# Linear attention feeding a SoLU layer on one core: the hand-written order of 907 pieces replaced by another

## The chip, the cores and the metric

The kernel runs on one core of one Trainium2 chip. What counts is the device time of one execution in microseconds (us). The core's engines each work through a queue of their own, in order: TensorE (PE in the profile, its weight loads PEld), VectorE (DVE), ScalarE (ACT), GpSimd (POOL) and SyncE (SP, which here only issues transfers). Transfers run on 16 DMA engines, whoever issues them.

## The reference

```python
q, k, v: (8, 8, 576, 64)            # batch, heads, sequence, head_dim, float32
kv  = einsum('bhsd,bhse->bhde', k, v)
o   = einsum('bhsd,bhde->bhse', q, kv)
a   = o / sqrt(mean(o * o, -1) + 1e-6) * g_norm
x   = a.transpose(0, 2, 1, 3).reshape(4608, 512)
h   = x @ w_in                      # 512 -> 1024
sm  = exp(h - max h) / (sum + 1e-9)
u   = h * sm                        # SoLU
ln  = (u - mean u) / sqrt(var u + 1e-6) * g_ln
out = ln @ w_out                    # 1024 -> 512, float32
```

## The kernel before, in words

The 4608 tokens are cut into nine chunks of 512. Chunk c from 0 to 7 holds eight of each nine tokens of batch c; chunk 8 gathers the ninth ones of all batches (`q_last`). The work on every chunk is cut into small pieces with names such as `h.3.5.0`; the first number is the chunk, or the batch.

The attention pieces: `kv_mm` (L375, PE) multiplies k by v, and `kv` copies (L229) bring the result from PSUM to SBUF in three parts, one of them whole and two shifted by half the partitions. `qT_mm` (L427, PE) turns q, and `qT` copies it out; from chunk 4 on, `qT` is instead one transposing transfer that SP issues (L435). `o_mm` (L448, PE) multiplies the turned q by kv, for two halves `hf` of the heads. `sq` (L233, ACT) squares o, `oa` (L460) adds two quarters of the squares, `s_mm` (L465, PE) averages them over a head, `ln` and `ex` (L472 and L476, ACT) make one over the root of it (for chunk 0 a single `ex`, L482), and `x` (L489, DVE, two instructions each) multiplies o by this and by g_norm.

The SoLU pieces: `h` (L532, PE) is a product with a slice of 128 columns of w_in, four matmuls of 512 columns. For chunks 0 to 2 it comes in two pieces of two matmuls (called halves below), so that the first can run when half of x is there. `exp` (L539, ACT) and `u` (L543, DVE, h times exp h) follow; no maximum is subtracted, and the division by the sum of exps is folded into the final scaling. `usq` (L233 on ACT or L235 on POOL) squares u, `es` (L551, POOL) adds two e. `ua`, `usqa` and `esa` (L575, DVE) fold eight slices of u, of its squares, and the four of es, to fewer; `sums` (L594, PE) adds what is left over the columns; `turn`, `stats` (L601 to L611, DVE) and `rstd` (L615, L617, ACT) make the scaling of each token. `out` (L651, PE) is the product with w_out, which has been centered once (`w_mean` on PE, `w_center` on DVE, L632 and L638). `ob` (L239 on ACT, L241 on DVE) scales it out of PSUM, and `store` brings it to memory: 256 KB a piece. The last piece, `out.8.3`, is done by halves of its columns (L659).

`warm` pieces (L300, PE) are products of zeros that nobody reads; `WARM` tells how many matmuls each has.

Nothing schedules this but the text in `ORDER`: `Plan.emit` takes its words one by one and emits the piece, so every engine gets its instructions in the order of the words. A word may name the engine (`:act`, `:pool`); without it a piece goes to the first engine allowed for it: DVE for `kv`, `qT`, `oa` and `ob`, POOL for `usq` and `es`, SP for `store`. The digits of `ROOMS` tell which of the 8 PSUM banks, or which SBUF buffer, each tile takes, in the order of first use; a tile waits until all users of the one before it in that room are done. `Plan.run` adds waits of its own:

```python
        if engine == "pool":
            self.after(ins, self.adds)
            self.adds.clear()
        if name[0] in ("ua", "usqa", "esa", "oa") and engine == "dve":
            self.adds.append(ins)
        elif name[0] in ("k", "v", "q", "q_last", "w_in", "w_out") and engine == "pool":
            self.after(ins, self.turns)
            ...
        elif name[0] == "qT" and engine == "sp":
            self.after(ins, self.loads[-2:-1])
```

So a piece on POOL waits for the adds of DVE that stand ahead of it in the order, a load issued by POOL for the transposing transfers ahead of it, and a transposing transfer for a load.

Loads of q, k, v and the weights are issued by POOL, which converts to bfloat16 on the way (L322, L338, L343, L348). Half of batch 0's v and k comes as float32 through SP (`wide`, L328) and is converted by ACT (`v.0.1`, `k.0.1`). `ident` (POOL) builds the unit matrices for the turns.

Of the kernel before, what the change touches and what calls it, by code (L numbers as in the profile page):

```python
# [30 lines left out]
u.0.7 sq.1.1.0 es.0.3 h.0.5.1 u.0.4 sq.1.1.1 h.1.0.0 w_mean.0 usq.0.1:act oa.1.1 u.0.0 exp.0.5 s_mm.1.1 ln.1.1 ex.1.1
u.0.5 es.0.2 w_mean.1 w_mean.2 w_mean.3 w_mean.4 w_mean.5 w_mean.6 usq.0.5:act x.1.1.1 usq.0.2 usq.0.7:act w_mean.7
x.1.1.0 usq.0.0 q.4.0 usq.0.4:act w_center.5 h.1.3.0 qT_mm.2.1 h.1.7.0 w_center.1 h.1.4.0 h.1.7.1 qT.2.1:act q.5.0
w_center.4 h.1.0.1 v.4.0 w_center.0 exp.1.7 qT_mm.2.0 exp.1.0 w_center.3 h.1.1.0 h.1.1.1 k.4.0 qT.2.0:act w_center.2
h.1.2.1 es.0.1 u.1.7 h.1.3.1 exp.1.1 h.1.4.1 u.1.0 exp.1.3 out.0.2.0 es.1.0 usq.0.3 u.1.1 exp.1.2 out.0.2.1 kv_mm.2.0
w_center.7 exp.1.4 h.1.5.0 w_center.6 kv.2.1.0:act kv.2.0.0:act h.1.5.1 kv.2.0.2:act kv.2.1.1 kv.2.0.1:act es.1.1
u.1.4 out.0.2.2 kv.2.1.2:act exp.1.5 o_mm.2.0 u.1.3 o_mm.2.1 sq.2.0.1 out.0.2.3 usq.1.1 u.1.2 qT_mm.3.0 sq.2.0.0 u.1.5
out.0.0.0 sq.2.1.1 oa.2.0 out.0.0.1 sq.2.1.0 qT.3.0 s_mm.2.0 usq.1.5 out.0.0.2 ln.2.0 qT_mm.3.1 oa.2.1:pool ex.2.0
h.1.6.0 qT.3.1 out.0.0.3 usq.1.2:act x.2.0.0 x.2.0.1 h.1.6.1 s_mm.2.1 exp.1.6 sums.0 usq.1.7 ln.2.1 u.1.6 ex.2.1
# [696 lines left out]
```

## Time and profile before

| | us |
|---|---|
| median of 3 runs | 177.52 (177.48 to 177.98) |
| span of the profiled execution | 175.8 |
| busy: PE, DVE, ACT, POOL | 164.2, 145.5, 152.1, 99.8 |
| DMA | 30.27 MB moved, 172 GB/s in the mean |

The profile is of one execution, in which no time but the span is given; the time of a run is larger than the span by what lies before the first and behind the last instruction (177.52 - 175.8 = 1.7 if that execution took the median). Its lines read: source line, engine, operation, what is written `<-` what is read, the number of instructions, then busy time, mean ns of one, and idle time of the engine ahead of them with what ended it. In the timeline a line begins with start and duration in us. A table of stretches gives for each engine its busy time in the stretch, then the clock granted to TensorE (1.00 is full), the busy share of the DMA engines and the GB/s that they moved. Matmuls overlap in their pipeline, so their durations in the timeline are longer than their distance.

### The profile page before, as it was taken

Reading aid. Unit: us, or ns where it says so; the run is one execution under the profiler, and the core shown is the slowest. Engines: PE = TensorE matmul, PEld = TensorE weight load, DVE = VectorE, ACT = ScalarE, POOL = GpSimd, SP = SyncE. Lnnn points to the kernel's source line nnn. Section 1 sums busy time; section 2 is a strip of 40 time slices with the busy share of each in tenths; the row PEclk is TensorE's granted clock in tenths of the full one; section 3 lists DMA queues with packets and bytes.
Section 4 is the critical chain, followed back from the end, with each engine's and each line's share of the span. In section 5 each row is a group of like instructions: output and inputs, shape, how many; then the busy total and the mean of one; then the engine's idle time right before and its main releaser. Section 6 shows DMA issues by size and latency. Waiting matters only on the chain.

```text
span 175.8 us, 4843 instructions
## 1 busy us (share of the span) xinstructions
PE 164.2 (93%) x1913; PEld 80.3 (46%) x1938; DVE 145.5 (83%) x317; ACT 152.1 (86%) x273; POOL 99.8 (57%) x108
## 2 busy tenths in 40 slices
...
GB/s 179 218 203 214 206 275 373 209 208 208 208 210 210 218 210 129 127 206 235 205 183 259 150 52 193 156 73 93 195 206 105 5 118 126 2 60 93 196 213 159
DMA packets 34623, 30.27 MB, mean 172 GB/s; under 512 B 16288, under 2 KB 28328, under 8 KB 34600
## 3 DMA queue, kind: packets, MB, share of 16 engines
...
q8 instruction: 15, 0.25, 0.6%
...
HBM read 32.51 MB, written 9.44 MB: 239 GB/s over the span
## 4 chain that ended last, share of the span: by engine, by line
PE 75%; DVE 10%; ACT 5%; DMA 5%; issue 2%; POOL 1%; POOLq 0%; DVEq 0%; ACTq 0%
PE h_ps L532 31%; PE out_ps L651 30%; DMA k_sb<-in_k_dram 5%; PE kv_ps L375 4%; PE o_ps L448 3%; DVE u_sb L543 3%; PE sum_ps L594 3%; PE s_ps L465 3%; DVE x_sb L489 2%; DVE w_out_sb L638 2%; ACT osq_sb L233 2%; DVE osq_sb L460 1%; PE out_ps L659 1%; ACT e_sb L539 1%; ACT kvd L229 1%
## 5 line engine op out<-in xcount | busy, mean ns | idle before, releaser
L532 PE MATMUL h_ps<-x_sb,w_in_sb 128*128 128x512 bf16 x280 | 68.0, 379 | 0.5
L651 PE MATMUL out_ps<-w_out_sb,u_sb 128*128 128x512 bf16 x266 | 65.2, 379 | 0.7 <-issue 0.3
L551 POOL TENSOR_TENSOR es_sb<-e_sb 128x512 bf16<-128x512 f32 x36 | 45.4, 1279 | 33.5 <-ACT e_sb L539 13.0
L539 ACT ACTIVATE e_sb<-h_ps,zero_t 128x512 f32<-128x512 f32 x72 | 46.2, 690 | 2.3 <-PE h_ps L532 1.7
L543 DVE TENSOR_TENSOR u_sb<-h_ps,e_sb 128x512 bf16<-128x512 f32 x72 | 46.6, 684 | 1.3 <-ACT e_sb L539 1.0
L532 PEld LDWEIGHTS <-w_in_sb 128*128 128x128 bf16 x288 | 27.3, 98 | 32.5 <-issue 1.3
L651 PEld LDWEIGHTS <-u_sb 128*128 128x128 bf16 x280 | 26.4, 98 | 31.6 <-issue 1.0
L233 ACT ACTIVATE usq_sb<-u_sb,zero_t 128x512 bf16<-128x512 bf16 x49 | 33.6, 718 | 0.0
L489 DVE SCALAR_TENSOR_TENSOR x_sb<-o_ps,g_sb,rst_sb 128x256 bf16<-128x256 f32 x72 | 30.2, 478 | 3.1 <-ACT rst_sb L476 2.5
L235 POOL TENSOR_TENSOR usq_sb<-u_sb 128x512 bf16<-128x512 bf16 x23 | 23.6, 1043 | 7.9 <-DVE osq_sb L460 5.6
L233 ACT ACTIVATE osq_sb<-o_ps,zero_t 128x512 bf16<-128x512 f32 x36 | 22.8, 689 | 3.5 <-PE o_ps L448 3.4
L239 ACT ACTIVATE ob_sb<-out_ps,rstd 128x512 f32<-128x512 f32 x22 | 14.8, 684 | 4.0 <-PE out_ps L651 3.8
L575 DVE TENSOR_TENSOR usq_sb<-usq_sb 128x2048 bf16<-128x2048 bf16 (+2 forms) x20 | 17.0, 848 | 0.6 <-ACT usq_sb L233 0.4
L229 DVE CAST kvd<-kv_ps 64x128 bf16<-64x128 f32 (+3 forms) x26 | 6.4, 256 | 11.2 <-ACT kvd L229 6.5
L241 DVE TENSOR_SCALAR ob_sb<-out_ps,rstd 128x512 f32<-128x512 f32 (+1 forms) x15 | 10.6, 711 | 4.1 <-PE out_ps L659 2.2
L322 POOL DMA_DIRECT2D v_sb<-in_v_dram x9 | 6.8, 757 | 10.1 <-DVE sum_ps L601 2.8
L472 ACT ACTIVATE lss_sb<-s_ps,eps_t 128x512 f32<-128x512 f32 x16 | 11.1, 695 | 1.0 <-PE s_ps L465 0.7
L476 ACT ACTIVATE rst_sb<-lss_sb,zero_t 128x512 f32<-128x512 f32 x16 | 11.5, 722 | 0.4
L375 PE MATMUL kv_ps<-v_sb,k_sb 64*64 64x64 bf16 x576 | 8.0, 194 | 2.8 <-DMA k_sb<-in_k_dram 1.3
L300 PE MATMUL warm_ps<-zeros 128*128 128x512 bf16 x25 | 8.8, 481 | 1.4 <-DVE zeros L255 1.2
L229 ACT CAST kvd<-kv_ps 64x128 bf16<-64x128 f32 (+3 forms) x34 | 8.2, 243 | 2.2 <-PE kv_ps L375 1.5
L375 PEld LDWEIGHTS <-k_sb 64*64 64x64 bf16 x576 | 6.8, 107 | 6.8 <-DMA k_sb<-in_k_dram 2.6
...
## 6 DMA issues: line engine op xcount, KB each, us to landing
...
q_sb<-in_q_dram POOLq DMA_DIRECT2D x6, 512.0 KB, 16.2
...
```

Of the source, the lines that this page charges most:

```text
L229: nc.scalar.copy(dst, src) if engine == "act" else on[engine].tensor_copy(dst, src)
L233: nc.scalar.activation(out=dst, in_=src, func=AF.Square, bias=zero_t[:, :])
L235: on[engine].tensor_tensor(out=dst, in0=src, in1=src, op=MUL)
L239: nc.scalar.activation(out=dst, in_=src, func=AF.Copy, scale=by)
L375: nc.tensor.matmul(t[64 * y:64 * y + 64, :], T["k", b][rows, n, i, :], T["v", b][rows, n, i, :], start=(i == 0 and (b < 2 or m == 0)), sto ...
L489: nc.vector.scalar_tensor_tensor(out=t[:, 2 * hf + dh, z], in0=T["o", c, hf, z][:, dh], scalar=g_rep[dh], in1=T["rst", c, hf][:, z], op0=M ...
L532: nc.tensor.matmul(bank(("h", c, f), [128, 512])[:, :], w_in_sb[:, dt, f * 128:(f + 1) * 128], T["x", c][:, dt].rearrange("p a b c -> p (a ...
L539: nc.scalar.activation(out=t[:, f % 2, :], in_=T["h", c, f][:, :], func=AF.Exp, bias=zero_t[:, :])
L543: nc.vector.tensor_tensor(out=t[:, f, :], in0=T["h", c, f][:, :], in1=T["e", c, f // 2][:, f % 2, :], op=MUL)
L551: on[engine].tensor_tensor(out=t[:, n, :], in0=e[:, 0, :], in1=e[:, 1, :], op=ADD)
L575: nc.vector.tensor_tensor(out=to[:, 0:n, :], in0=src[:, 0:n, :], in1=src[:, n:2 * n, :], op=ADD)
L651: nc.tensor.matmul(bank(("out", c, m), [128, d_model])[:, :], T["u", c][:, f, m * 128:(m + 1) * 128], w_out_sb[:, f, :], start=(f == 0), s ...
```

## The change

The three texts are replaced; the functions stay. The same 907 pieces are emitted in another order, with other rooms. The seven `warm` pieces have 45 matmuls instead of 27. Another engine is named for 73 pieces:

| pieces | from, to | from, to |
|---|---|---|
| `usq` | ACT to POOL 17 | POOL to ACT 11 |
| `kv` copies | ACT to DVE 15 | DVE to ACT 12 |
| `oa` | DVE to POOL 5 | POOL to DVE 1 |
| `ob` | ACT to DVE 4 | DVE to ACT 3 |
| `qT` copies | ACT to DVE 2 | DVE to ACT 1 |
| last stores | `store.8.2` ACT to SP | `store.8.0` SP to ACT |

POOL issues its 40 loads in the same succession, and so does SP its own, but for `store.8.2` in the place of `store.8.0`. `ident` moves behind the first three loads of POOL. The diff, cut to its core (the old order's lines first):

```diff
 ORDER = """
-wide.v ident wide.k g_rows q.0.1 v.0.0 k.0.0 q.0.0 v.0.1:act v.1.0 k.1.0 q.1.0 w_in.0 k.0.1:act w_in.1 warm.0
-kv_mm.0.1.0 qT_mm.0.1 kv.0.1.0.0:act kv.0.1.1.0 kv_mm.0.1.1 q.1.1 qT.0.1:act kv.0.1.2.1 kv.0.1.2.0 kv.0.1.1.1
-kv.0.1.0.1:act warm.1 kv_mm.0.0.0 v.1.1 kv_mm.0.0.1 o_mm.0.1 kv.0.0.0.1 sq.0.1.1 warm.2 qT_mm.0.0 k.1.1 kv.0.0.1.0:act
-kv.0.0.2.0:act kv.0.0.1.1:act kv.0.0.0.0:act qT.0.0 kv.0.0.2.1:act sq.0.1.0 warm.3 o_mm.0.0 w_out.0 turn_g sq.0.0.0
-s_mm.0.1 g_mean sq.0.0.1 warm.4 kv_mm.1.0.1 w_out.1 ex.0.1 kv_mm.1.0.0 kv.1.0.2.1 s_mm.0.0 kv.1.0.2.0 kv.1.0.0.1:act
-kv.1.0.0.0 kv.1.0.1.1 kv.1.0.1.0 qT_mm.1.0 ex.0.0 q.2.0 qT.1.0:act x.0.0.0 x.0.0.1 warm.5 o_mm.1.0 sq.1.0.0 warm.6
-h.0.6.0 h.0.3.0 k.2.0 sq.1.0.1 x.0.1.0 table h.0.0.0 oa.1.0 x.0.1.1 s_mm.1.0 h.0.2.0 h.0.7.0 h.0.2.1 ln.1.0 v.2.0
...
-kv_mm.3.0 es.1.2 turn.0 stats.0 out.0.3.0 kv.3.1.0:act x.2.1.0 x.2.1.1 usq.1.0:act out.0.3.1 usq.1.4 usq.1.3 h.2.6.0
-out.0.3.2 rstd.0 h.2.0.0 ob.0.0:act usq.1.6 kv.3.0.1 ob.0.2 h.2.6.1 kv.3.1.2:act kv.3.0.0:act kv.3.1.1:act out.0.3.3
-usqa.1.0 kv.3.0.2:act h.2.4.0 exp.2.6 h.2.5.0 ob.0.3:act ua.1.0 o_mm.3.0 h.2.1.0 store.0.3 sq.3.0.0 h.2.0.1 sq.3.0.1
...
-exp.5.2 u.5.0 h.5.4.0 rstd.3 es.5.1 x.6.1.1 usq.4.4:act out.3.1.0 ob.3.0 exp.5.4 es.5.3 h.6.6.0 usq.4.3:act ob.3.3
-usq.4.0:act u.5.4 h.6.3.0 exp.5.5 ua.4.1 h.5.1.0 usq.4.1:act u.5.5 q_last.0 exp.6.6 out.3.1.1 u.5.2 q_last.4
...
-store.6.2 stats.7 usq.8.2:act out.7.2.0 ua.8.0 ob.6.1:act usq.8.5:act usq.8.4:act store.6.1 out.7.0.1 rstd.7
-ob.7.0:act usqa.8.0 out.8.2.0 ob.7.3:act out.7.2.1 store.7.0 usqa.8.1 out.8.0.0 usqa.8.2 ob.7.2:act ua.8.1 store.7.3
-esa.8.0 store.7.2 ua.8.2 out.7.1.0 out.7.1.1 sums.8 ob.7.1:act out.8.2.1 turn.8 stats.8 store.7.1 out.8.0.1 out.8.1.0
-out.8.1.1 out.8.3.0 rstd.8 ob.8.2:act ob.8.0 store.8.2:act store.8.0 ob.8.1:act store.8.1:act ob.8.3.0 store.8.3.0
-out.8.3.1 ob.8.3.1 store.8.3.1:act
+wide.v wide.k g_rows q.0.1 v.0.0 k.0.0 ident q.0.0 v.1.0 k.1.0 q.1.0 w_in.0 w_in.1 q.1.1 warm.0 qT_mm.0.1 v.1.1 k.1.1
+w_out.0 warm.1 kv_mm.0.0.1 kv.0.0.0.1 kv_mm.0.0.0 kv.0.0.0.0 v.0.1:act k.0.1:act kv_mm.0.1.1 kv_mm.0.1.0 kv.0.1.0.0
+kv.0.1.0.1 kv.0.1.2.1 kv.0.0.2.1:act w_out.1 q.2.0 k.2.0 v.2.0 kv.0.0.2.0 kv.0.0.1.1 kv.0.0.1.0 kv.0.1.1.0:act
+qT_mm.0.0 qT.0.0:act warm.2 o_mm.0.0 turn_g qT.0.1 kv.0.1.2.0 kv.0.1.1.1 o_mm.0.1 sq.0.0.0 sq.0.0.1 kv_mm.1.0.1
+kv.1.0.1.1 kv.1.0.2.1 g_mean kv.1.0.0.1:act sq.0.1.1 kv_mm.1.0.0 s_mm.0.0 kv.1.0.1.0 ex.0.0 sq.0.1.0 kv.1.0.2.0:act
+kv.1.0.0.0:act x.0.0.0 warm.3 qT_mm.1.0 qT.1.0 s_mm.0.1 warm.4 o_mm.1.0 x.0.0.1 warm.5 h.0.1.0 h.0.0.0 ex.0.1 x.0.1.0
+sq.1.0.1 sq.1.0.0 h.0.5.0 h.0.6.0 x.0.1.1 oa.1.0 s_mm.1.0 table ln.1.0 ex.1.0 h.0.4.0 h.0.1.1 h.0.0.1 exp.0.1 h.0.4.1
+x.1.0.0 u.0.1 h.0.6.1 exp.0.0 u.0.0 exp.0.4 exp.0.6 h.0.5.1 h.0.2.0 exp.0.5 q.3.0 v.3.0 k.3.0 x.1.0.1 usq.0.0 qT_mm.1.1
+qT.1.1 h.0.2.1 h.0.7.0 kv_mm.1.1.1 kv.1.1.1.1 kv_mm.1.1.0 exp.0.2 kv.1.1.0.1:act es.0.2 kv.1.1.2.1:act kv.1.1.2.0:act
+kv.1.1.1.0 kv.1.1.0.0 warm.6 o_mm.1.1 u.0.6 u.0.5 u.0.2 h.0.7.1 h.0.3.0 h.0.3.1 sq.1.1.1 sq.1.1.0 w_mean.0 exp.0.7
+oa.1.1 u.0.4 h.1.7.0 exp.0.3 u.0.3 s_mm.1.1 ln.1.1 usq.0.1 w_mean.1 h.1.0.0 w_mean.2 w_mean.3 ex.1.1 u.0.7 es.0.0
+usq.0.7:act usq.0.4:act h.1.1.0 x.1.1.1 x.1.1.0 w_mean.4 h.1.2.0 usq.0.5 w_mean.5 w_mean.6 w_mean.7 es.0.3 w_center.1
+w_center.0 w_center.2 h.1.4.0 h.1.4.1 qT_mm.2.1 exp.1.4 qT.2.1:act u.1.4 w_center.6 es.0.1 h.1.2.1 h.1.0.1 exp.1.0
+w_center.5 h.1.7.1 exp.1.7 u.1.7 exp.1.2 u.1.0 w_center.3 h.1.5.0 h.1.5.1 h.1.1.1 out.0.0.0 exp.1.1 h.1.6.0 q.4.0 q.5.0
+v.4.0 usq.0.6 qT_mm.2.0 k.4.0 exp.1.5 es.1.2 qT.2.0:act u.1.5 w_center.4 usq.0.2 h.1.6.1 h.1.3.0 out.0.0.1 h.1.3.1
+exp.1.6 es.1.3 kv_mm.2.0 exp.1.3 kv.2.1.2:act out.0.0.2 w_center.7 kv.2.0.2:act kv.2.1.1:act out.0.0.3 u.1.1 u.1.6
+u.1.3 kv.2.0.1:act out.0.2.0 usq.1.5 kv.2.1.0:act kv.2.0.0:act o_mm.2.0 usq.0.3:act o_mm.2.1 u.1.2 qT_mm.3.1 sq.2.0.0
+qT.3.1 out.0.2.1 qT_mm.3.0 sq.2.0.1 out.0.2.2 oa.2.0 s_mm.2.0 sq.2.1.1 qT.3.0 sq.2.1.0 oa.2.1 out.0.2.3 ua.1.0 ln.2.0
+ex.2.0 x.2.0.1 out.0.3.0 out.0.3.1 s_mm.2.1 ln.2.1 x.2.0.0 usq.1.4 ex.2.1 out.0.3.2 usq.1.0 usq.1.7:act es.1.0
+out.0.3.3 x.2.1.1 x.2.1.0 sums.0 turn.0 kv_mm.3.0 usq.1.1 usq.1.3 kv.3.1.2 h.2.1.0 kv.3.1.1 usq.1.6:act usq.1.2:act
+stats.0 kv.3.0.0 kv.3.0.1:act kv.3.1.0:act h.2.1.1 exp.2.1 kv.3.0.2:act h.2.4.0 h.2.0.0 h.2.0.1 o_mm.3.0 rstd.0 u.2.1
+ua.1.1 h.2.2.0 h.2.2.1 exp.2.0 u.2.0 sq.3.0.0 ob.0.0:act h.2.4.1 h.2.3.0 ob.0.2 exp.2.2 ob.0.3:act h.2.5.0 es.1.1
+h.2.3.1 h.2.5.1 h.2.6.0 h.2.7.0 usqa.1.0 usqa.1.1 sq.3.0.1 oa.3.0:pool u.2.2 usq.2.2 h.2.6.1 exp.2.4 exp.2.5 u.2.4
+exp.2.3 h.2.7.1 exp.2.7 u.2.5 usq.2.5 es.2.2 u.2.7 exp.2.6 out.0.1.0 s_mm.3.0 ln.3.0 out.0.1.1 ex.3.0 u.2.6 store.0.3
...
+usq.4.4:act ln.6.1 ex.6.1 out.3.0.1 ua.4.0 usq.4.1 h.5.0.0 usq.4.2 ua.4.1 sq.6.0.1 out.3.3.0 out.3.3.1 x.6.1.0 rstd.3
+ob.3.3 out.3.1.0 out.3.1.1 sq.6.0.0 oa.6.0 exp.5.0 s_mm.6.0 ln.6.0 ex.6.0 x.6.1.1 u.5.0 h.5.2.0 exp.5.2 es.5.1 es.5.3
+ob.3.0 h.5.1.0 exp.5.1 h.5.4.0 exp.5.4 x.6.0.0 usq.5.0:act x.6.0.1 u.5.2 usq.4.0:act h.5.5.0 exp.5.5 es.5.2 u.5.4
+es.5.0 usq.5.4:act h.6.4.0 h.6.3.0 exp.6.3 h.6.7.0 exp.6.7 u.5.1 u.5.5 exp.6.4 h.6.5.0 h.6.1.0 u.6.3 kv_mm.7.0 exp.6.5
...
+usq.8.6:act usq.8.3:act usq.8.7:act ob.6.0:act usq.8.0:act store.5.3 store.6.3 store.6.0 ua.7.2 usqa.7.2 sums.7 turn.7
+usq.8.4:act usq.8.1:act usq.8.5:act stats.7 rstd.7 ob.7.2:act ob.6.2 store.6.2 store.6.1 out.7.3.1 out.8.3.0 out.7.0.0
+out.7.0.1 out.8.0.1 out.7.1.0 es.8.3 es.8.0 usqa.8.0 esa.8.0 usqa.8.1 usqa.8.2 ua.8.0 out.8.2.0 out.7.1.1 ua.8.1 ua.8.2
+sums.8 ob.7.0:act ob.7.3:act store.7.0 out.8.1.0 out.8.1.1 store.7.3 ob.7.1:act store.7.2 turn.8 stats.8 rstd.8
+ob.8.1:act out.8.2.1 out.8.3.1 ob.8.0 ob.8.2 store.7.1 store.8.2 store.8.0:act ob.8.3.0 store.8.1:act store.8.3.0
+ob.8.3.1:act store.8.3.1:act
 """
...
 ROOMS = """
-0100001110123045670021342251106330561121035621422317002110311036052473601734320610036472100126013114216047201351060316
...
+0100001110021123412005065263400011700060756512111374010010124022061253065271346001712500323162513141106471645301010000
...
 """
...
 WARM = """
-14 3 1 3 1 4 1
+21 11 5 3 1 2 2
 """
```

More of the change, by code (lines that the diff above doesn't have):

```diff
@@ L31 @@
[L31 to L39, printed above, removed]
-kv_mm.3.0 es.1.2 turn.0 stats.0 out.0.3.0 kv.3.1.0:act x.2.1.0 x.2.1.1 usq.1.0:act out.0.3.1 usq.1.4 usq.1.3 h.2.6.0
```

83 lines of the change are left out of this document (37 added, 46 removed).

## The prediction

> **What bounds the kernel now.** I read the page's head first, then busy time by stretch, cut at 19.84 (the first h product) and at 46.
>
> ```profile
> span 175.8 us, 4843 instructions
> ```
>
> ```profile
> 0.00:19.84 19.84, 14.83 (x212) 7.41 (x215) 6.53 (x33) 11.19 (x20) 11.59 (x23) 1.00 1.02 205
> 19.84:46.00 26.16, 24.00 (x277) 12.58 (x282) 22.47 (x43) 24.52 (x44) 20.31 (x22) 1.00 1.22 246
> 46.00:172.50 126.50, 125.32 (x1430) 60.35 (x1443) 116.06 (x242) 116.35 (x211) 67.86 (x64) 1.00 0.81 152
> ```
>
> The second column is the length, the third PE's busy time. After 46 PE is idle for 126.50 - 125.32 = 1.18 us in all, between 19.84 and 46 for 2.16. So TensorE's in-order work bounds the kernel from the first h product on. What stands ahead of that product is the same in both orders (the kv products of batches 0 and 1's first half, the three transposes, three o products, two s products and the turn of g, beside the zero-products), so the end is: time of the first h product, plus the same work, plus the idle behind it, plus what follows PE's last product. At most 2.16 + 1.18 = 3.3 us of idle can go; a worse order has no such floor.
>
> The profiled execution spans 175.8 us and the median of the runs is 177.52, so 1.7 us lie around the span. I sum in the span and add 1.7.
>
> **The start.** In the timeline, columns are start and duration:
>
> ```profile
> 0.74 0.20 POOL masks.py:197 MEMSET ident<- 128x128 bf16 x1 [0.29 <-POOLq L720]
> ...
> 1.20 5.29 PE L300 MATMUL warm_ps<-zeros 128*128 128x512 bf16 x14 [1.20 <-DVE zeros L255]
> ...
> 1.63 0.89 POOL L322 DMA_DIRECT2D q_sb<-in_q_dram  x1
> ...
> 11.26 0.76 PE L375 MATMUL kv_ps<-v_sb,k_sb 64*64 64x64 bf16 x36 [1.31 <-DMA k_sb<-in_k_dram]
> ```
>
> ```profile
> 19.83 0.98 PEld L532 LDWEIGHTS <-w_in_sb 128*128 128x128 bf16 x6 [0.27 <-DMA w_in_sb<-in_moe_w_in_dram]
> ```
>
> ```profile
> 2.00:3.00 1.00, 1.00 (x4) 0.42 (x3) 0.08 (x5) 0.02 (x1) 1.00 (x2) 1.00 0.72 212
> ```
>
> `ident` now stands behind three load issues, so POOL's first load is issued 1.63 - 0.74 = 0.9 us sooner. The DMA engines are busy 0.72 of the time between 2 and 3 us already (second column from the right), so only the rest, some 0.3 us, and a little before 2 can become earlier data: I take 0.35 us for every early load (bounds 0 and 0.9). The successions are kept, except that two of the last stores exchange their queues.
>
> The prices, from the page's groups (busy, mean ns) and, for single shapes, the groups by form:
>
> ```profile
> L539 ACT ACTIVATE e_sb<-h_ps,zero_t 128x512 f32<-128x512 f32 x72 | 46.2, 690 | 2.3 <-PE h_ps L532 1.7
> L543 DVE TENSOR_TENSOR u_sb<-h_ps,e_sb 128x512 bf16<-128x512 f32 x72 | 46.6, 684 | 1.3 <-ACT e_sb L539 1.0
> ...
> L233 ACT ACTIVATE usq_sb<-u_sb,zero_t 128x512 bf16<-128x512 bf16 x49 | 33.6, 718 | 0.0
> L489 DVE SCALAR_TENSOR_TENSOR x_sb<-o_ps,g_sb,rst_sb 128x256 bf16<-128x256 f32 x72 | 30.2, 478 | 3.1 <-ACT rst_sb L476 2.5
> L235 POOL TENSOR_TENSOR usq_sb<-u_sb 128x512 bf16<-128x512 bf16 x23 | 23.6, 1043 | 7.9 <-DVE osq_sb L460 5.6
> L233 ACT ACTIVATE osq_sb<-o_ps,zero_t 128x512 bf16<-128x512 f32 x36 | 22.8, 689 | 3.5 <-PE o_ps L448 3.4
> ...
> L229 DVE CAST kvd<-kv_ps 64x128 bf16<-64x128 f32 (+3 forms) x26 | 6.4, 256 | 11.2 <-ACT kvd L229 6.5
> ...
> L476 ACT ACTIVATE rst_sb<-lss_sb,zero_t 128x512 f32<-128x512 f32 x16 | 11.5, 722 | 0.4
> ...
> L229 ACT CAST kvd<-kv_ps 64x128 bf16<-64x128 f32 (+3 forms) x34 | 8.2, 243 | 2.2 <-PE kv_ps L375 1.5
> ```
>
> ```profile
> L575 DVE TENSOR_TENSOR usq_sb<-usq_sb 128x2048 bf16<-128x2048 bf16 x8 | 9.8, 1219 | 0.4 <-ACT usq_sb L233 0.4
> ...
> L460 DVE TENSOR_TENSOR osq_sb<-osq_sb 128x512 bf16<-128x512 bf16 x15 | 6.7, 445 | 1.0 <-ACT osq_sb L233 0.6
> ...
> L229 ACT COPY qT_sb<-qt_ps 128x1024 bf16<-128x1024 bf16 x4 | 4.0, 1012 | 0.9 <-PE qt_ps L427 0.9
> ...
> L229 DVE COPY qT_sb<-qt_ps 128x1024 bf16<-128x1024 bf16 x4 | 2.8, 688 | 1.6 <-PE qt_ps L427 1.6
> ...
> L460 POOL TENSOR_TENSOR osq_sb<-osq_sb 128x512 bf16<-128x512 bf16 x1 | 1.1, 1150 | 0.0
> ```
>
> and PE's pace, from the chain: 6.91 / 32 = 0.216 us for a 512-column product.
>
> ```profile
> 70.35 6.91 PE h_ps L532 x32
> ```
>
> The new order, walked: `warm.0` has 7 more products, 1.20 + 5.29 + 7 x 0.216 = 8.0. `qT_mm.0.1` and 11 zero-products bring PE to 10.85, when k.0.0 arrives (11.26 - 0.35 = 10.9). The zero-products fill waiting for data and cost nothing; if data came sooner, they would cost up to 11 x 0.216 = 2.4. Four kv products of 18 (0.35 each, half of the 36 above) end at 12.3. DVE then makes six copies (6 x 0.26) to 13.9, ACT the copy `qT.0.0` (1.01) to 13.9, and `o_mm.0.0` runs at 14.0 to 14.4. ACT: two squares (2 x 0.69) to 15.8, the copy `kv.1.0.0.1` behind `kv_mm.1.0.1` to 16.2, `sq.0.1.1` to 16.9, `ex.0.0` to 17.6. DVE: `x.0.0.0` (2 x 30.2 / 72 = 0.84) to 18.45, then `qT.1.0`, which moved to DVE (0.69, before: 1.01 on ACT), then `x.0.0.1` to 20.0. The first h product needs both x: 20.0. w_in.0, which it waited for at 19.84, is no longer the last. **+0.2** (-0.4, if the walk is late by all that the data gain, to +0.6).
>
> **19.84 to 46.** These waits make 1.79 of the 2.16 us:
>
> ```profile
> 31.08 0.38 PE L465 MATMUL s_ps<-osq_sb,head_mean 128*128 128x512 bf16 x1 [0.71 <-DVE osq_sb L460]
> ...
> 34.08 0.62 PE L427 MATMUL qt_ps<-ident,q_sb 128*128 128x128 bf16 x8 [0.57 <-DMA q_sb<-in_q_dram]
> ...
> 40.40 0.77 PE L375 MATMUL kv_ps<-v_sb,k_sb 64*64 64x64 bf16 x72 [0.51 <-DVE u_sb L543]
> ```
>
> All three go: `s_mm.1.1` has one more half h (2 x 0.216 = 0.43) between it and its o product, three halves stand among the w_mean products, and `qT_mm.2.1` and `kv_mm.2.0` come 1.3 and 1.8 us of PE work later. New ones come. `oa.1.0` (0.445) now stands behind `x.0.1.1`, so `s_mm.1.0` waits: four h halves end at 20.0 + 1.7, two x and the oa at 20.0 + 1.7 + 0.4, so 0.4. `qT_mm.2.0` takes bank 4, which frees with `u.1.7`, and DVE does two centerings before that: 0.35. All six kv.2 copies are on ACT (6 x 0.24), one was on DVE: `o_mm.2.0` waits 0.25 more. `out.0.2.0` waits 0.2 for `u.1.1`. The two products of `warm.6` lie in the wait for the kv.1.1 copies. -1.79 + 1.2 = **-0.6** (-1.8 to +0.5).
>
> **46 to 60.** DVE's queue now has the first fold of u.1 (1.22, as the usq row) ahead of all four x.2, then three kv.3 copies (before one, 2 x 0.26 more), then `u.2.1`. And `h.2.2.0` takes the very bank of `h.2.1`: between them PE has h.2.4.0, h.2.0.0, h.2.0.1 and an o product, 3 x 0.43 + 0.36 = 1.66, while exp and u alone take 0.69 + 0.65 = 1.34, and u stands behind what is left of that queue. The fold is mostly in a wait for `ex.2.0`; I take **+0.4** (0 to +1.5, the fold and one link of the bank's chain late).
>
> **60 to 166.** The exchange of engines: 17 squares leave ACT for POOL and 11 come back, a net of 6; four oa net go from DVE to POOL. POOL +6 x 1.04 + 4 x 1.15 = +10.8; ACT -6 x 0.72, less a `qT` copy, three kv copies and one scaling, about -6.7; DVE +0.4. PE idles 1.18 us here, so ACT's relief can't be worth more than that, and I take 0. POOL's loads stand behind these operations: k.3.0 now stands ahead of a square, q.4.0 behind one operation more (1.04), with loads long under way. Queued behind the POOL oa's waits for DVE's folds are only squares, sums and loads due many us later. One place is tighter: from `s_mm.6.0` to `h.6.4.0` PE has four h of 0.864, 3.46 (before: five, 4.3), and the chain is ln and exp (2 x 0.72) and two x on DVE (2 x 0.84), 3.1, with `ob.3.0` (about 0.7) before them: 3.8. **+0.3** (-1.1, nearly all the idle there, to +0.8).
>
> **The end.**
>
> ```profile
> 166.89 0.34 PE sum_ps L594 x16
> ...
> 172.57 0.48 DVE ob_sb L241
> ```
>
> ```profile
> 168.60 0.30 ACT L617 ACTIVATE rstd<-lv,zero_t 128x4 f32<-128x4 f32 x1
> ...
> 169.64 0.38 ACTq L675 DMA_DIRECT2D out_dram<-ob_sb  x1
> ...
> 171.54 1.89 ACTq L675 DMA_DIRECT2D out_dram<-ob_sb  x2
> ```
>
> ```profile
> 170.00:170.50 0.50, 0.50 (x4) 0.27 (x3) 0.00 (x0) 0.00 (x0) 0.00 (x0) 1.00 0.05 12
> ...
> 171.00:171.50 0.50, 0.50 (x8) 0.44 (x5) 0.00 (x0) 0.50 (x1) 0.00 (x0) 1.00 1.05 402
> ...
> 174.00:174.50 0.50, 0.00 (x0) 0.00 (x0) 0.00 (x0) 0.00 (x0) 0.00 (x0) 1.00 0.67 234
> ```
>
> Before, six pieces of 0.86 follow `sums.8`; now four, so rstd.8, 2.0 us behind the sums, is there 1.9 us before PE's end instead of 3.7. All last 1 MB of stores (256 KB three times, 128 KB twice) waits for it. At 402 GB/s (last column) that takes 2.6 us. Before, the first of them was issued at 169.64 and its data began past 170.5, 0.9 later; now its issue can't be sooner than the scaling behind rstd.8 allows, 1.0 before PE's end. So the data end 2.5 us after PE, where before they ended at about 174.4, 1.9 after PE's 172.55. **+0.5** (0, if the stores overlap better, to +0.7).
>
> Sum: +0.2 - 0.6 + 0.4 + 0.3 + 0.5 = +0.8: span 176.6, time **178.3**. By the bounds 174.2 to 181.6 at once; they will not all fall together, so I take the forecast's own range as 177.0 to 179.4.
>
> **Rivals.** *Faster:* the early waits go (-1.8) and nothing is given back: the reuse of a bank after 1.66 us of PE work is met as the old order's closest one (1.9, counted in its lists) was, and the stores cost 0.3. With the start's 0.2: -1.8 + 0.2 + 0.3 = -1.3, 176.2. For it: 1.18 us idle in 126 says that tight distances are mostly met. Against: DVE is busy 22.47 of 26.16 there, and the list above. Chance 0.27.
>
> *Much slower, through POOL and DVE:*
>
> ```profile
> 28.21 2.52 POOL L551 TENSOR_TENSOR es_sb<-e_sb 128x512 bf16<-128x512 f32 x2
> ...
> 30.23 0.79 DVE L460 TENSOR_TENSOR osq_sb<-osq_sb 128x512 bf16<-128x512 bf16 x1
> ```
>
> This add took 0.79 us, its 15 fellows 0.445 in the mean, and it began while POOL was summing e until 30.73. POOL work is ordered behind DVE's adds, but an add may meet POOL work that has begun. POOL gets ten operations more; if seven of them met an add at 0.35 each, 2.4 us would come into DVE's queue, and from the point where DVE and not PE is last that is the kernel's: 180.0. Against: only one such add is seen in 15. Chance 0.15. The Trainium skill's page "SBUF — State Buffer", section "Who interferes with whom", states this as a rule: a DVE operation with two SBUF inputs and a POOL operation that reads SBUF exclude each other for the whole instruction. The 0.79 agrees. By the rule in full, each of the ten could block an add for its whole length, 10.8 us and a time near 188; the trace is far from that.
>
> **How the numbers follow.** The forecast has 0.58. A measurement tells about 0.3%, 0.53 us, from no change. Of the forecast's 0.58 I put 0.27 within that and 0.31 above; with the rivals: faster 0.27, same 0.27, slower 0.46. The range reaches into half of each rival: 176.1 to 180.0.
>
> **What would show it.** First h product at 20.0 with x as releaser, not w_in; the three quoted waits gone; new waits of PE at `h.2.2.0` and at h.6 on DVE's u and x; PE idle after 46 above 1.18; PE's end to the span's end longer than the 3.2 us of now (175.8 - 172.57). I am wrong if PE's idle behind the first h falls below 2.7 us, or the last stores end no later after PE; or, on the other side, if the adds of DVE stretch.

## The result, and the profile after

The changed kernel takes 186.72 us in the median (185.94 to 187.43, 4 runs), the kernel before on the same chip 177.51 (177.48 to 177.98): a ratio of 1.052, 95% interval 1.049 to 1.0551. It is 9.2 us slower. The prediction said 178.3 and 176.1 to 180.0. The profiled execution took 186.61, with a span of 184.8. Of one kernel below, the kernel before with a late load, two of eight executions were slow (181.1 and 181.35, the others 178.17 to 179.53), and its time and ratio are of the other six.

Busy time by stretch of the changed kernel (length, then PE, PEld, DVE, ACT, POOL, granted clock, DMA share, GB/s); 19.78 is its first h product, PE's last product ends at 180.8:

```profile
span 184.8 us, 4923 instructions
```

```profile
19.78:46.00 26.22, 25.36 (x288) 13.00 (x287) 23.08 (x45) 23.36 (x43) 20.23 (x21) 1.00 1.22 246
46.00:180.80 134.80, 126.57 (x1440) 59.45 (x1438) 117.09 (x238) 112.97 (x204) 78.83 (x74) 1.00 0.76 139
46.00:60.00 14.00, 12.46 (x214) 6.10 (x212) 12.24 (x28) 11.96 (x24) 7.60 (x7) 1.00 1.03 178
60.00:86.00 26.00, 25.45 (x355) 11.93 (x354) 23.64 (x52) 23.71 (x45) 21.63 (x22) 1.00 1.06 191
86.00:102.00 16.00, 13.23 (x180) 6.00 (x182) 12.47 (x27) 13.44 (x25) 7.17 (x8) 1.00 0.80 128
```

PE is idle for 26.22 - 25.36 = 0.86 us up to 46 (before 2.16) and for 134.80 - 126.57 = 8.23 from there (before 1.18). So the first part is 1.3 better and the rest 7.05 worse. From PE's end to the span's end it is 4.0 (before 3.25). That makes 6.4 of the 9.0 by which the span grew. The rest I put down to stops that the records hide: a product's record lasts 0.38 us in the rows below, PE's pace is 0.216, and so a stop can hide up to 0.16. The large stops, in PE's timeline (start, duration, idle time before and what ended it):

```profile
53.47 1.02 PE L531 MATMUL h_ps<-x_sb,w_in_sb 128*128 128x512 bf16 x4 [1.50 <-ACT kvd L228]
...
100.73 1.02 PE L531 MATMUL h_ps<-x_sb,w_in_sb 128*128 128x512 bf16 x4 [2.62 <-DVE u_sb L542]
102.61 0.65 PE L447 MATMUL o_ps<-qT_sb,kvd 64*32 64x256 bf16 x32 [0.29 <-DMA qT_sb<-q_sb]
111.32 0.38 PE L464 MATMUL s_ps<-osq_sb,head_mean 128*128 128x512 bf16 x1 [0.83 <-DVE osq_sb L459]
...
133.06 0.38 PE L464 MATMUL s_ps<-osq_sb,head_mean 128*128 128x512 bf16 x1 [1.70 <-ACT ob_sb L238]
```

Each releaser was itself waiting. These two waits of ACT in the changed kernel (in all, times, longest) are not in the list of the kernel before:

```profile
ACT kvd L228 <- DVE kvd L228: 7.5, 6, 4.0
ACT ob_sb L238 <- DMA out_dram<-ob_sb: 7.0, 6, 2.3
```

The first is a copy of a kv bank that waits until DVE has done its copy of the same bank, the second a scaling whose result buffer is still being stored. Behind the stop at 100.73 the chain reads, on ACT and then on DVE:

```profile
98.59 0.69 ACT L238 ACTIVATE ob_sb<-out_ps,rstd 128x512 f32<-128x512 f32 x1 [2.00 <-DMA out_dram<-ob_sb]
99.30 0.26 ACT L228 CAST kvd<-kv_ps 64x128 bf16<-64x128 f32 x1
```

```profile
99.59 0.49 DVE L228 CAST kvd<-kv_ps 128x128 bf16<-128x128 f32 x2 [2.75 <-ACT kvd L228]
100.00 0.68 DVE L542 TENSOR_TENSOR u_sb<-h_ps,e_sb 128x512 bf16<-128x512 f32 x1
```

`ob.2.1` waits on ACT for a buffer, `kv.6.1.2` stands behind it, DVE's `kv.6.1.0` waits for that copy, `u.4.2` stands behind, and `h.5.3.0` takes the bank that `u.4.2` reads.

### The profile page after: what moved, and what is told of

Same layout as the page of the kernel before. It is cut to its first block, busy times and chain, and to the rows that moved or that the text cites. A ratio compares the mean times of both kernels' runs of the same rounds, so it can differ in the third digit from the quotient of the medians.

```text
span 184.8 us, 4923 instructions
## 1 busy us (share of the span) xinstructions
PE 169.6 (92%) x1956; PEld 81.4 (44%) x1956; DVE 148.1 (80%) x318; ACT 146.3 (79%) x262; POOL 110.6 (60%) x118
## 4 chain that ended last, share of the span: by engine, by line
PE 53%; DMA 14%; ACT 11%; DVE 11%; SPq 4%; issue 3%; POOL 2%; POOLq 0%; ACTq 0%; DVEq 0%
PE h_ps L531 23%; PE out_ps L650 18%; DMA qT_sb<-q_sb 7%; DMA q_sb<-in_q_dram 4%; DMA out_dram<-ob_sb 3%; DVE x_sb L488 3%; ACT osq_sb L232 3%; SPq L678 3%; PE o_ps L447 3%; ACT kvd L228 2%; PE kv_ps L374 2%; PE warm_ps L299 2%; ACT e_sb L538 2%; DVE kvd L228 1%; PE s_ps L464 1%
## 5 line engine op out<-in xcount | busy, mean ns | idle before, releaser
L650 PE MATMUL out_ps<-w_out_sb,u_sb 128*128 128x512 bf16 x280 | 66.1, 379 | 0.0
L234 POOL TENSOR_TENSOR usq_sb<-u_sb 128x512 bf16<-128x512 bf16 x29 | 30.2, 1051 | 12.1 <-DVE ua_sb L574 7.8
L232 ACT ACTIVATE usq_sb<-u_sb,zero_t 128x512 bf16<-128x512 bf16 x43 | 29.1, 716 | 0.0
L238 ACT ACTIVATE ob_sb<-out_ps,rstd 128x512 f32<-128x512 f32 (+1 forms) x21 | 14.1, 677 | 10.5 <-DMA out_dram<-ob_sb 7.0
L228 DVE CAST kvd<-kv_ps 64x64 bf16<-64x64 f32 (+3 forms) x29 | 6.9, 251 | 14.5 <-PE kv_ps L374 10.6
L240 DVE TENSOR_SCALAR ob_sb<-out_ps,rstd 128x512 f32<-128x512 f32 (+1 forms) x16 | 11.7, 730 | 5.6 <-PE out_ps L650 2.5
L228 ACT CAST kvd<-kv_ps 64x128 bf16<-64x128 f32 (+3 forms) x31 | 7.1, 247 | 8.4 <-DVE kvd L228 7.5
L299 PE MATMUL warm_ps<-zeros 128*128 128x512 bf16 x45 | 12.5, 422 | 1.3 <-DVE zeros L254 1.2
L321 POOL DMA_DIRECT2D q_sb<-in_q_dram x10 | 7.7, 766 | 6.9 <-DVE osq_sb L459 3.1
L464 PE MATMUL s_ps<-osq_sb,head_mean 128*128 128x512 bf16 x20 | 7.2, 378 | 3.4 <-ACT ob_sb L238 1.9
```

Source lines behind the costliest of these rows:

```text
L228: nc.scalar.copy(dst, src) if engine == "act" else on[engine].tensor_copy(dst, src)
L232: nc.scalar.activation(out=dst, in_=src, func=AF.Square, bias=zero_t[:, :])
L234: on[engine].tensor_tensor(out=dst, in0=src, in1=src, op=MUL)
L299: nc.tensor.matmul(t[:, :], zeros[:, 0:128], zeros[:, :], start=True, stop=True)
L321: nc.gpsimd.dma_start(t.rearrange("p n j d -> p n (j d)")[:, hs.start // 2:hs.stop // 2], rows_of(src, b, hs, js))
L650: nc.tensor.matmul(bank(("out", c, m), [128, d_model])[:, :], T["u", c][:, f, m * 128:(m + 1) * 128], w_out_sb[:, f, :], start=(f == 0), s ...
```

## The experiments

The first three theories came from these rows. S: the stores kept in their old succession hold the four result buffers. K: the kv copies that are split over ACT and DVE. P: the work given to POOL.

A row with SPq or ACTq is the issuing of transfers by that engine, and its duration is how long the issue held the engine's queue.

**Eight result buffers.**

```diff
-        "u": 4, "ua": 1, "usq": 2, "es": 2, "ob": 4,
+        "u": 4, "ua": 1, "usq": 2, "es": 2, "ob": 8,
```

> The changed kernel with eight result buffers (ob) in place of four and nothing else. Theory S (the stores kept in their old succession hold the four result buffers, and ACT's scalings wait for them in ACT's queue): the six waits of ACT's ob for a DMA, 7.0 us together, go or shrink to under 1 us; with them the stalls of PE at 100.7 (2.6 us) and 133 (1.7 us) and about half of the longer end, so the time falls from 186.7 to 181.5 to 183.5. Theory K (copies of one kv bank split over ACT and DVE wait for each other, in whatever queue they stand) leaves those stalls: 186 to 187, with the waits for the DMA gone but PE still stopped at 53.5 and 100.7. Theory P (squares and sums on POOL slow DVE and come late) likewise: 186 to 187.

Measured: 186.94, ratio 1.0524 (1.0492 to 1.0556), no change. PE's stop at 100.7 is down to 0.56, and another stands some 2 us later in PE's waits:

```profile
PE o_ps L447 <- DMA qT_sb<-q_sb: 2.4, 1, 2.4
```

Theory S fell in the form that it had; the transposed q.6 was late as well.

**Stores directly behind their scalings.**

```diff
-rstd.4 ob.4.3:act ob.4.1:act out.4.2.0
+rstd.4 ob.4.3:act store.4.3 ob.4.1:act store.4.1 out.4.2.0
```

> The changed kernel with each store directly behind its scaling in the order, so that the succession of transfers on SP's queue follows that of the scalings; four result buffers as before. Theory S: the same as with eight buffers, 181.5 to 183.5, and no wait of an ob for a DMA above 0.5 us except at the end. If the buffers were too few in themselves (four that are held for the 2 us of a transfer), this one stays nearer to 186 than eight buffers do. Theories K and P: 186 to 187.

Measured: 190.05 (1.0701, 1.0667 to 1.0734), 3.3 us worse, which none of the three theories had. In this order SP's transposing transfers stand behind stores that wait for their scaling; PE waited 2.7 us for the transposed `q_last`, and 3.3 at an h.

**Old engines for the kv copies** (27 pieces), and, in a kernel of its own, **for squares and their sums** (34 pieces).

```diff
-kv.3.1.2 h.2.1.0 kv.3.1.1
+kv.3.1.2:act h.2.1.0 kv.3.1.1:act
```

> The changed kernel with the 27 copies of kv that changed engine put back on the engine that they had before; order, squares and sums as changed. Theory K: PE's stall at 53.5 (1.5 us) goes, since the copy on ACT need not wait for one behind x and the turn on DVE, and the 2.75 us wait of kv.6.1.0 for kv.6.1.2 at 99.6 goes: 183 to 184.5. Theory S: within 0.7 of 186.7, since ACT's queue is still held by the scalings that wait for a store. Theory P: the same 186 to 187.

```diff
-usq.0.1
+usq.0.1:act
...
-oa.2.1
+oa.2.1:pool
```

> The changed kernel with the 28 squares of u and the 6 sums of squares that changed engine put back on the engine that they had before; order, copies and scalings as changed. POOL loses some 10 us of work, ACT gains some 8. Theory P (POOL's added work stretches DVE's two-input operations, as the sum at 109.5 that took 1.74 us where others took 0.42, and comes late for the sums): 2 us or more back, 183 to 185. Theories S and K: 186 to 188, for the ob waits and split copies stay and ACT has more to do.

Measured: 191.63 (1.0775) and 193.81 (1.0912), so 4.9 and 7.1 us slower. K expected a gain from the first and P from the second, and no theory a loss of this size. So in this order neither part can be undone as a whole.

The two losses are made in different places. With the old squares the first h product runs at 19.80, as in the changed kernel, and the loss lies behind it. With the old copies it runs at 23.97 in place of 19.78, so 4.2 of the 5.5 us by which this profiled span is longer (190.3 against 184.8) stand ahead of it. The copy `kv.0.0.0.0` is back on ACT, ahead of `v.0.1`, and waits there for its product; the conversion of v, at 5.14 in the changed kernel, waits behind it, and PE waits for that of k. The changed kernel, then two rows of ACT and one of PE with the old copies:

```profile
5.14 1.15 ACT L228 CAST v_sb<-u_sb 128x1152 bf16<-128x1152 f32 x1 [3.12 <-DMA u_sb<-in_v_dram]
```

```profile
12.02 0.21 ACT L229 CAST kvd<-kv_ps 128x64 bf16<-128x64 f32 x1 [9.99 <-PE kv_ps L375]
12.12 1.15 ACT L229 CAST v_sb<-u_sb 128x1152 bf16<-128x1152 f32 x1
```

```profile
14.38 0.76 PE L375 MATMUL kv_ps<-v_sb,k_sb 64*64 64x64 bf16 x36 [2.40 <-ACT k_sb L229]
```

So by its trace most of what the old copies cost is one copy in the wrong place, with a lower clock behind that stop (last section); the run says little of the other 26.

**Old and new joined, and the engines alone.** The changed order's first 242 pieces and then the rest in the old order; the mirror of it; and the old order with all 73 new engines.

```diff
 ua.1.0 ln.2.0 ex.2.0
-x.2.0.1 out.0.3.0 out.0.3.1
+es.1.0 es.1.1 usq.1.1
```

> The changed kernel up to its first exponent of block 2 (242 pieces, some 48 us), with its zero-products and its engines, and behind them the pieces that are left in the order and on the engines of the kernel before. Theory L (the loss is made by the order behind 46 us alone, and the early part is a gain of 1.3 us of PE's idle time): 176.0 to 176.8, faster than before. Theory G (the early part's gain is bought by work put off, which comes due later): 177.5 or more. Theory E (the engines of the copies and squares cost, wherever they stand): 177.5 to 179, for the early part has its share of the changed engines.

```diff
 h.1.6.0 qT.3.1 out.0.0.3
-usq.1.2:act x.2.0.0 x.2.0.1
+es.1.2 h.1.6.1 exp.1.6
```

> The mirror of the run before: the kernel before up to its last product of block 2 that fits (239 pieces), and behind them the pieces that are left in the changed order and on the changed engines. Theory L: 187.5 to 188.5 (the late part's loss without the early part's gain of 1.3). Theory G: 185 to 186.5. Theory E: 185 to 187.

```diff
-usq.0.1:act oa.1.1 u.0.0
+usq.0.1 oa.1.1 u.0.0
```

> The kernel before, in its own order and rooms, with the 73 pieces that changed engine on their new engine. Theory E: most of the 9 us, 183 or more. Theory L (the order makes the loss): some loss is left, for each order was written for its own engines, but less than half of it, 178 to 181.

Measured: 180.31 (1.0162, 1.0132 to 1.0192), 191.28 (1.0759) and 189.09 (1.0662). Theory L missed all three: the early part's gain did not survive the seam, and both joined kernels cost more than their parts. Theory G met the first and missed the second, theory E missed both. A seam leaves pieces undone that either order had done by then (in the second, PE stops 3.13 us for an x at 51.8, close behind it), so these two add little to what PE's idle time shows above, that the loss is made behind 46 us. On the third, theory E was right: the engines alone cost 11.6 us in the old order.

**The load of q.7.** In both orders POOL issues its loads in the same succession, but not at the same time. POOL's timeline of the kernel before, then of the changed one:

```profile
82.45 0.80 POOL L322 DMA_DIRECT2D q_sb<-in_q_dram  x1
```

```profile
91.66 0.81 POOL L321 DMA_DIRECT2D q_sb<-in_q_dram  x1 [3.14 <-DVE osq_sb L459]
```

This load is 9.2 us later. The load of k.6 ahead of it is 3.9 us later already (81.04, before 77.19); between the two stand five squares and sums of POOL (before, two), and an `oa` of DVE for which POOL waits. What it meets, first before, then after (length 4 us; the DMA share and GB/s are the last columns):

```profile
90.00:94.00 4.00, 3.95 (x87) 2.10 (x87) 3.86 (x11) 3.98 (x8) 4.00 (x4) 1.00 0.86 200
```

```profile
90.00:94.00 4.00, 4.00 (x20) 1.75 (x19) 3.72 (x9) 3.94 (x7) 2.33 (x3) 1.00 0.20 13
94.00:98.00 4.00, 4.00 (x88) 1.96 (x86) 2.63 (x5) 2.59 (x5) 1.75 (x2) 1.00 1.07 201
```

The DMA engines are nearly empty when the load should run, and full when the stores and the transposing transfers come. The landing of the stores issued from 86 to 102 us, before and after, and SP's transposes of q.6 and q.7, before and after:

```profile
DMA to landing us min/median/max: 2.3/2.4/2.6
```

```profile
DMA to landing us min/median/max: 5.1/5.2/5.4
```

```profile
91.37 3.66 SPq L435 DMA_TRANSPOSE qT_sb<-q_sb  x2
```

```profile
95.00 7.21 SPq L434 DMA_TRANSPOSE qT_sb<-q_sb  x2
```

So both victims, the buffer that frees late and the q.6 that comes late, would have one cause. The Trainium skill's page "DMA: Bandwidth & Descriptors", section "Issuing engines are not separate DMA queues", says that transfers started by ScalarE, SyncE or GpSimd run on the same 16 DMA engines and interleave. The landings of 5.2 us in place of 2.4, of stores that SP issued beside a load that POOL issued, agree. The test is one word, with eight buffers and with four:

```diff
-exp.4.5 k.6.0 h.4.3.0 kv_mm.5.0
+exp.4.5 k.6.0 q.7.0 h.4.3.0 kv_mm.5.0
...
-oa.5.0 ln.5.1 q.7.0 ex.5.1
+oa.5.0 ln.5.1 ex.5.1
```

> The changed kernel with eight result buffers and with the load of q.7 directly behind that of k.6 in the order, some 9 us earlier on POOL's queue, near where the kernel before has it. With eight buffers alone, PE's stop at 100.7 went over to a wait for the transposed q.6 at 102 (2.41 us), whose transfer runs beside the late load of q.7. If two covers hid each other there, this run gives the 2.4 us back: 184 to 185. If a third chain (the split copies of kv.6) is due at the same place, it stays at 186 to 187.

> The changed kernel with four result buffers as it has them, and only the load of q.7 moved up behind that of k.6. If the two waits near 100 us cover each other (a scaling that waits for a result buffer on ACT, and the transposed q.6 that comes late), taking one away alone brings little, as eight buffers alone brought nothing: 186 to 187. If the late load of q.7 was the whole of it, this run gives what both gave together: 184 to 184.7.

Measured: 184.03 (1.0373, 1.033 to 1.0415) with eight, 183.56 (1.0335, 1.0309 to 1.036) with four. The first is what I expected of two waits that cover each other; the second shows one cause instead: the word alone gives 3.2 us back, the buffers nothing. In the run with four buffers the load is issued at 81.59, the stores land in 2.4 us again, ACT's wait near 98 is gone, and PE's stop there is 0.51:

```profile
98.39 1.02 PE L531 MATMUL h_ps<-x_sb,w_in_sb 128*128 128x512 bf16 x4 [0.51 <-DVE u_sb L542]
```

**Three more repairs, one upon the other** (on the kernel with eight buffers and early q.7), and the first two of them with four buffers:

```diff
-ob.8.3.1:act store.8.3.1:act
+ob.8.3.1:dve store.8.3.1:act
...
-stats.0 kv.3.0.0 kv.3.0.1:act
+stats.0 kv.3.0.0:act kv.3.0.1:act
...
-exp.5.5 es.5.2 u.5.4 es.5.0 usq.5.4:act
+exp.5.5 es.5.2 q_last.0 q_last.4 u.5.4 es.5.0 q_last.6 q_last.2 q_last.5 usq.5.4:act
```

> The run with eight buffers and the early q.7 (184.0), with the last half-tile's scaling on DVE, where the kernel before has it, in place of ACT. On ACT it stood behind two stores that ACT issues itself, whose issue took 2.84 us there, and the span ended 5.1 us behind PE's last product. On DVE it follows its product: the end 3.3 to 4 us behind PE as before, so 182.3 to 183.1. If the two stores' issue is what ends last, whatever engine scales, it stays at 184.

> The same with one copy more on its old engine: kv.3.0.0 on ACT, so that ACT's copy of the same bank does not wait for DVE, which is at x and the statistics. PE's stop of 1.5 us at 54 shrinks to 0.5 or less. If what is won there stays: 181 to 182. If the next wait takes it back (every later piece is as late on its own engine as PE is), within 0.5 of the run before.

> The same with the last five pieces of q_last loaded some 5 us earlier on POOL's queue, so that the transposed q.8 is there when the products o of the last block want it; PE waited 0.72 for it at 134.5. If that wait is the bound there: 180.3 to 181.5. If the folds and scalings around 130 us are as late, or POOL's squares come later behind the loads: no change or 0.5 slower.

> The changed kernel with its four result buffers and three repairs: the early q.7, the last half-tile's scaling on DVE, and the copy kv.3.0.0 on ACT. With eight buffers the same three gave 182.5, with PE's last product at 176.3 and 5.0 us from there to the end, of which 2.37 is the issue of the first of ACT's stores; with four buffers and early q.7 alone that end was 4.0 us. If the eight buffers themselves lengthen the end (more stores in flight when ACT issues its own): 181.2 to 181.9. If the end stays at 5 us: 182.3 to 182.8. If ACT's scalings wait for buffers near 130 us again and PE behind them: 182.5 to 183.5.

Measured: 182.78 (1.0304, 1.0267 to 1.0341), 182.51 (1.0273), 183.35 (1.0319); with four buffers 182.51 (1.0292, 1.0267 to 1.0318). The intervals of neighbours in this row overlap, so no single repair of the three is clear of the noise in time; what each did is read from the traces.

The scaling on DVE did not do what I expected, though the time fell into the range: the end stayed 5.0 us long (181.2 - 176.2). ACT's three stores, in the run with eight buffers and the scaling on DVE, and in the one with four (durations of one issue, min, median, max in ns):

```profile
L674 ACTq DMA_DIRECT2D out_dram<-ob_sb x3: 404/408/2367, 175.1 to 178.1; - x3
```

```profile
L674 ACTq DMA_DIRECT2D out_dram<-ob_sb x3: 339/376/518, 175.8 to 178.1; - x3
```

One issue of 2.37 us holds the last store on ACT's queue, whoever scales; with four buffers it is not there, and the end is 3.9 us (180.8 - 176.9). The same 2.34 to 2.37 us stand in all five runs with eight buffers, and in none with four. The 1.2 us that the run was faster than the one with eight buffers and early q.7 came ahead of PE's end, and I can't put it down to the edit: 0.75 of it lies ahead of the first h product (19.83 against 20.58), where the two kernels are the same. The kv copy did what theory K says of that one stop, 1.50 to 0.40, but the time stayed within 0.5 of the run before, as expected if the next wait takes it back:

```profile
52.93 1.02 PE L531 MATMUL h_ps<-x_sb,w_in_sb 128*128 128x512 bf16 x4 [0.40 <-ACT kvd L228]
```

With four buffers PE's end came 0.9 us sooner by the two repairs together (176.9 against 177.8 with early q.7 alone) and the time is 1.05 lower by the medians, 0.8 by the ratios, whose intervals just meet. The early `q_last` brought nothing; a stop of 1.13 at an h came in its place at 120.5. With four buffers this stop is left (`s_mm.7.0` takes the bank that `ob.4.3` reads, and that scaling waits for a result buffer):

```profile
129.45 0.38 PE L464 MATMUL s_ps<-osq_sb,head_mean 128*128 128x512 bf16 x1 [1.34 <-ACT ob_sb L238]
```

**The zero-products.**

```diff
-21 11 5 3 1 2 2
+14 3 1 3 1 4 1
```

> The changed kernel with the zero-products of the kernel before (27 in place of 45), nothing else. They stand where PE has nothing else to do: the first h follows x at 19.8 in both kernels. So the same, 185.9 to 187.4. If PE runs slower where fewer of them go ahead (a granted clock under 1.00 in the first 20 us or a later first h): 0.5 to 2 us slower. If the 18 more of them are in the way of real work (4 us of PE): 1 us or more faster.

Measured: 186.53 (1.0499, 1.0445 to 1.0552), no change. The granted clock was 1.00 all through the first 20 us, with fewer of them too. As far as an interval of 1 us to either side tells, this part of the change is free.

**The order alone, and the old order with the new squares.**

```diff
-kv.3.0.0 kv.3.0.1:act
+kv.3.0.0:act kv.3.0.1
...
-usq.0.1
+usq.0.1:act
```

> The changed order, zero-products and rooms, with all 73 pieces on the engine that they had before: the fourth of the square, of which old order with old engines is 177.5, old order with new engines 189.1, new order with new engines 186.7. If order and engines cost independently, 186.7 less 11.6 makes 175.1. If each order needs its own engines, as the runs with the old kv engines (191.6) and the old square engines (193.8) in the new order say: 194 to 199.

```diff
-usq.0.1:act oa.1.1 u.0.0
+usq.0.1 oa.1.1 u.0.0
```

> The kernel before with only the 28 squares and 6 sums of squares on their new engine; kv copies, transposes and scalings on the old. If POOL's added squares and sums are what the new engines cost in the old order (sums on POOL that PE waits for at 58.6 and 73.7, 1.8 us, and DVE's sums slow beside POOL), it takes most of the 11.8 us: 184 to 188. If the split kv copies are: 179 to 182.

Measured: 200.89 (1.1322, 1.1302 to 1.1343), even above what was expected if each order needs its own engines, and 185.76 (1.0461, 1.0434 to 1.0488), as expected if the squares and sums are the cost. The square, in us (order stands for order, rooms and zero-products together):

| | old engines | new engines |
|---|---|---|
| old order | 177.5 | 189.1 |
| new order | 200.9 | 186.7 |

Engines cost 11.6 in the old order and save 14.2 in the new; the order costs 23.4 with the old engines and saves 2.4 with the new. Neither has a price of its own. Some 3.9 of the 14.2 is the copy `kv.0.0.0.0` again (the order alone has its first h product at 23.67), and up to 3.4 us of the 200.9 is a lower clock (last section); the rest still has the opposite sign of the 11.6. What the rooms cost by themselves was not measured. In the old order the squares and sums make 8.3 of the 11.6. The groups of that run show two ways, ACT's exps that wait for room in `e` until POOL's `es` is done, and DVE's folds of the squares, whose mean went up from the 848 ns of the kernel before:

```profile
L539 ACT ACTIVATE e_sb<-h_ps,zero_t 128x512 f32<-128x512 f32 x72 | 46.6, 690 | 8.8 <-POOL es_sb L551 5.2 <-PE h_ps L532 2.3 <-DVE u_sb L543 1.0
```

```profile
L575 DVE TENSOR_TENSOR usq_sb<-usq_sb 128x2048 bf16<-128x2048 bf16 (+2 forms) x20 | 19.9, 995 | 2.1 <-POOL usq_sb L235 1.9
```

**One word in the kernel before**, twice: q.7 late, and `ident` behind the first loads.

```diff
-kv.5.1.2:act h.4.4.0 q.7.0 kv.5.0.2
+kv.5.1.2:act h.4.4.0 kv.5.0.2
...
-s_mm.5.0 es.4.2 store.2.3
+s_mm.5.0 es.4.2 q.7.0 store.2.3
```

> The kernel before with one word moved: the load of q.7 behind the sum es.4.2, some 9 to 10 us later on POOL's queue (82.45 there), which is its place in the changed order against the work around it. If the late load alone costs what its repair gave back (3.2 us), because the transposes and the stores behind them are held on SP: 179.5 to 181. If it costs only together with the new order's other late work: under 178.5.

```diff
-wide.v ident wide.k g_rows q.0.1 v.0.0 k.0.0 q.0.0
+wide.v wide.k g_rows q.0.1 v.0.0 k.0.0 ident q.0.0
```

> The kernel before with one word moved: the identity matrices built behind POOL's first three loads, as in the changed order, so that the loads are issued 0.38 us earlier (1.25 in place of 1.63). If the start of the chain to the first x is bound by these loads: 0.2 to 0.4 faster, 177.1 to 177.3. If it is bound by the wide loads on SP and their narrowing on ACT, or the transposes that need the identity come later: 177.5 or up to 0.4 slower.

Measured: 178.5 in the median of six, ratio 1.0061 (1.0039 to 1.0082), for the first, 1.1 us slower by the ratio. That is at the upper bound of the second expectation and well under the first. The load was issued at 89.14, so 6.7 us later and not the 9 to 10 expected, and SP and PE show:

```profile
90.62 7.82 SPq L435 DMA_TRANSPOSE qT_sb<-q_sb  x2
```

```profile
98.91 0.65 PE L448 MATMUL o_ps<-qT_sb,kvd 64*32 64x256 bf16 x32 [1.23 <-DMA qT_sb<-q_sb]
```

So the late load costs by itself one wait of 1.2 us; in the new order, 9.2 us late, it also found a scaling that needed the store's buffer, ahead of a kv copy that DVE wanted, and cost 3.2. The second: 177.21 against 177.46, ratio 0.9981 (0.9967 to 0.9995). It is the fastest kernel here, by 0.2%, less than the 0.3% set as a bound. That the earlier loads are the reason is not shown: its first h product is at 19.23, before at 19.84, but at 19.30 in the run with the late q.7, where `ident` stands as before.

## Why the prediction was wrong, and where it was right

- *First h product*, forecast at 20.0 with x ahead of it: 19.78, before 19.84. The zero-products cost nothing, as walked; the run with the old ones shows it. The 0.2 means nothing: in eight profiled kernels that are the same up to there (the changed one and those that differ only in buffers or behind it) this product starts between 19.78 and 20.69.
- *19.84 to 46*, -0.6: PE's idle fell by 1.3, within the bounds. The three quoted waits are gone, so that mechanism held. Of the four new waits that gave 1.2 back none shows; the one that does is 0.73 at 28.46, for the kv.1.1 copies, where the walk had put the two products of `warm.6`.
- *46 to 60*, +0.4 (0 to +1.5): idle 1.54 against 0.12 in the same stretch before, +1.4. The place was wrong. Not `h.2.2.0` on `u.2.1`, but `h.2.0.0` in the bank of `kv.3.1`, whose copy on ACT stood behind one that waited 1.80 for DVE. That the number lies within the bounds is luck.
- *60 to 166*, +0.3 (-1.1 to +0.8): this is the step that failed. PE's idle behind 60 is 6.7 us where it was 1.06, so 5.6 us came in the place of 0.3. The term put POOL's loads behind the exchanged work at nothing: it looked at k.3 and q.4, and called what is queued behind POOL's waits for DVE's folds "due many us later". It did not look at q.7, which waits behind squares, sums and an `oa` of DVE, came 9.2 us later and was due; the repair gives 3.2 us back. The price of the exchange of engines was taken from the engines' sums (ACT -6.7, POOL +10.8), and the square shows that such sums can't price it: the same exchange is worth +11.6 or -14.2. Waits of scalings for result buffers were not in the term at all, and one of them makes the stop of 1.70 at 133. At the one tight place that I named, `s_mm.6.0` to `h.6.4.0`, the stop stands at its start, 0.83 at `s_mm.6.0` (111.32), and none at the h.
- *The end*, +0.5 (0 to +0.7): +0.75, the size about right. The walk had no waits of the last scalings for result buffers, and `ob.8.3.1` had one of 1.22 us on ACT.
- *Rivals*: the slower side was right, but for another reason. The mechanism of the much slower rival, POOL in DVE's way, is there, but small in this order. In DVE's timeline:

```profile
109.52 1.74 DVE L459 TENSOR_TENSOR osq_sb<-osq_sb 128x512 bf16<-128x512 bf16 x1
```

This add is `oa.6.0`. It took 1.74 us against 0.445 in the mean before, while POOL issued loads and squared, and PE's 0.83 at 111.32 follows. DVE's ten other adds took 0.42 in the mean, and its folds of the squares 852 ns, before 848, so there was one meeting and not seven. That the measured time comes near the 188 of ten adds blocked in full is chance: all eleven adds together took 5.9 us, before fifteen took 6.7. In the old order with the new squares the folds did stretch (995 ns); that POOL's squares are why was not tested by itself.

So the runs show the cause of 3.2 us of the 9.2, the late load of q.7, and hardly more. What stays open is some 5 us, from 177.5 to the 182.5 of the repaired kernel. They are spread over stops of at most 1.34 us and many short ones, and the repair of one of these (`q_last`) gave nothing. That the rest is the looser fit of this order to its engines as a whole is argued from the square, not shown piece by piece.
